# Attention and two MLP layers on one core: split inputs kept in DRAM for the wide tiles, and six weight chunks decoded through PSUM

## The chip, the core and the metric

The kernel runs on one core of a Trainium2 chip. The metric is the device time in microseconds of one execution. Three timed runs of the kernel before took 1110.44, 1110.76 and 1112.65 us (median 1110.76). One more execution was profiled; it took 1110.38 us.

## The reference

Four batches of eight heads of attention (576 rows, 64 columns a head) are mixed with a linear memory term, and go through two MLP layers of 2304 tokens, 512 model columns and 2048 hidden columns:

```python
scores = where(causal, -1e9, q @ k.T / 8); a = softmax(scores)
q_p = elu(q) + 1
attn = sigmoid(beta) * (q_p @ M_prev) / (q_p . z_prev + 1e-6) + (1 - sigmoid(beta)) * (a @ v)
x = attn laid out as (2304, 512)
x1 = elu(x @ moe_w_in) @ moe_w_out
out = leaky_relu(x1 @ moe2_w_in) @ moe2_w_out
```

The MLP weights arrive as float64, read as pairs of 32-bit integers. Tokens and weights are each split into a high part and a low remainder, both of a type that TensorE takes in one pass, and a product is the sum of three matmuls: high by high, low by high, high by low.

## The kernel before

**Order.** The program is written in units (a tile of scores, one chunk of an MLP layer, a load). A scheduler that simulates the program with costs of its own fixes the order of the instructions on every engine when the kernel is built. On the chip each engine, and SyncE's queue, which issues all DMAs, then runs its list strictly in order.

**Weights.** The 2048 hidden columns are 16 chunks `f` of 128. `load_w` fetches a chunk's two integer blocks, `wraw` (512 KB each, two buffers), and makes the pair `w`. It has two forms. Where `pools["decode_bank"]` names a PSUM bank, it works on halves of 128x512 through that one bank: ScalarE L112, VectorE L113, L114, L117, ScalarE's cast (helper `copy`, L242), VectorE L121 for the low part. A half keeps the bank from its first step to its last, so the next half starts behind it. Otherwise it works on the whole chunk of 128x1024 in the SBUF tile `wm` (one buffer): ScalarE L126, VectorE L127, L128, L131, ScalarE's cast, and GpSimd L137 twice for the low part.

**Attention with the first layer's narrow part.** The first seven chunks (`NFA`) are decoded during the first batch, by the PSUM form through bank `po`. Tokens come in eight parts of 288 (`pi` 0 to 7). As soon as the attention of a batch is through, its two parts' units are woven into the attention of the next: `u_x` makes the input x of a part, `u_h` one chunk's hidden block (12 matmuls in a PSUM bank, then `elu`: ScalarE L631, L632, VectorE L633, and `g_split`: VectorE's cast to `gh`, L244, and GpSimd's `gl`, L626), `u_o` the seven chunks' share of the output, stored as `ys`. For parts 2 to 7 `u_x` loads two halves of x, adds them on VectorE (L682), stores the sum as `xs` (L683), and splits it (`split_x`): ScalarE casts `xh`, GpSimd subtracts `xl` (L612). Parts 0 and 1 have their x in `xm` already.

**Between attention and the wide part.** From about 410 us the last parts' units run, merged with the loads of six more chunks (`merge(side, wun[:NPRE])`, L782), which use the SBUF form. The remaining three are loaded inside the first wide tile.

**Wide part.** The nine other chunks, 7 to 15, run over tiles of 512 tokens (four, and one of 256). `load2` gets a tile's x 256 tokens at a time through the one buffer `x`, and splits it into `xw`, `xv`: ScalarE casts `xw` (L242) and GpSimd subtracts `xv` (L806). Two sets of `xw`, `xv` alternate. Hidden blocks go to banks `tp` and `pm` in turn (two of each, so the fifth chunk, f = 11, needs the bank that the ELU of f = 7 has read). The tile's four output blocks use three `sc` banks and `po`. At a tile's end VectorE adds `ys` (L852), and the sums are stored as `x1s` (L853) from the two buffers `st`. Then the second layer runs over all 16 chunks, with its own loads (L818) and the same `load_x`.

Of the kernel before, what the change touches and what calls it, by code (L numbers as in the profile page):

```python
# [8 lines left out]
F32 = mybir.dt.float32  # L9
F32R = mybir.dt.float32r  # L10
# [5 lines left out]
P = 128  # L16
# [3 lines left out]
def _f(ap):  # L20
    return ap.bitcast(F32)
# [3 lines left out]
def kernel(  # L25
# [14 lines left out]
    nc = tc.nc  # L40
# [4 lines left out]
    NKC = DM // P  # L45
# [6 lines left out]
    V32 = 1  # L52
# [7 lines left out]
    TN = 256  # L60
# [87 lines left out]
    def halves(n):  # L148
# [5 lines left out]
    xq_scr = [  # L154
        [dram.tile([P, NKC, tile_tok(t)[1]], F32, name=f"xq{i}_{j}") for j in range(2)] for i, t in enumerate(tiles1)
    ]
    x_scr = [
        xm_scr[t][:, :, o:o + w] if t < V32 else dram.tile([P, NKC, w], F32, name=f"xs{i}")
        for i, (t, o, w, _) in enumerate(parts)
    ]  # L160
    y_scr = [dram.tile([P, NKC, p[2]], F32, name=f"ys{i}") for i, p in enumerate(parts)]
    x1_scr = [dram.tile([P, NKC, TN], F32, name=f"x1s{i}") for i in range(NTT)]

# [497 lines left out]
    def phase1_units(ti):  # L661

        units = []
        for pi, (pt, o, w, _) in enumerate(parts):
            if pt != ti:
                continue
            st = {}

            def u_x(pi=pi, o=o, w=w, st=st):
                xt = mtile("x", 1, F32, (NKC, NW))[:, :, 0:w]  # L670
                if ti < V32:
                    nc.sync.dma_start(xt, xm_scr[ti][:, :, o:o + w])
                    st["x"] = split_x(xt, w, pi % 2)
                    st["g"] = {}
                    return
                x2 = mtile("y", 1, F32, (NKC, NW))[:, :, 0:w]
                for j in range(2):
                    ps, pz = slice(64 * j, 64 * j + 64), slice(64 - 64 * j, 128 - 64 * j)
                    nc.sync.dma_start(xt[ps], xq_scr[ti][j][ps, :, o:o + w])
                    nc.sync.dma_start(x2[ps], xq_scr[ti][j][pz, :, o:o + w])  # L680
                for c in range(NKC):
                    nc.vector.tensor_tensor(out=xt[:, c], in0=xt[:, c], in1=x2[:, c], op=ALU.add)  # L682
                nc.sync.dma_start(x_scr[pi], xt)  # L683
                st["x"] = split_x(xt, w, pi % 2)
                st["g"] = {}

            def u_h(f, w=w, st=st):
                ph = h_bank()[:, 0:w]
                h_mm(ph, wi_tiles[0, f], *st["x"])
                st["g"][f] = elu(ph, w)  # L690

            def u_o(ec, pi=pi, w=w, st=st):
                py = bank("sc" if tail else "pm")[:, 0:w]
                o_mm(py, range(NFA), 0, ec, st["g"], 0, NFA - 1)
                y = mtile("st", 2)[:, 0:w]
                copy(E_Y, y, py)
                nc.sync.dma_start(y_scr[pi][:, ec], y)

            units.append((0, u_x))
            for f in range(NFA):  # L700
                units.append((HC * 12 * w / 2.4, lambda f=f, u=u_h: u(f)))
            for ec in range(NKC):
                units.append((3 * NFA * w / 2.4, lambda ec=ec, u=u_o: u(ec)))
        return units
# [74 lines left out]

    wun = [(1, lambda f=f: load_w(0, wpb, w1i, w1o, f, f - NFA)) for f in range(NFA, NF)]  # L780
    tail = True
    merge(side, wun[:NPRE])  # L782
    wun = wun[NPRE:]
    w2 = [lambda f=f: load_w(1, wpa, w2i, w2o, f, f) for f in range(NFA)]
    w2 += [lambda f=f: load_w(1, wpb, w2i, w2o, f, f - NFA) for f in range(NFA, NF)]
# [5 lines left out]

    n_wide = 0

    def load_x(fetch, t0, n):

        nonlocal n_wide
        par = n_wide % 2
        n_wide += 1
        xh = mtile(f"xw{par}", 1, F32R, (NKC, TW))[:, :, 0:n]
        xl = mtile(f"xv{par}", 1, F32R, (NKC, TW))[:, :, 0:n]  # L800
        for o in range(0, n, TN):
            xt = mtile("x", 1, F32, (NKC, TN))
            fetch(xt, t0 + o)
# [8 lines left out]
    wide = [(t0, min(TW, NT - t0)) for t0 in range(0, NT, TW)]  # L812

    def load2(t0, n):
        return load_x(lambda xt, t: recut(xt, x_scr, t, TN), t0, n)

    def load3(t0, n):
        return load_x(lambda xt, t: nc.sync.dma_start(xt, x1_scr[t // TN]), t0, n)  # L818
# [104 lines left out]
```

## Time and profile before

| | kernel before |
|---|---|
| median of 3 runs, us | 1110.76 |
| profiled execution, us | 1110.38 |
| its span, first to last instruction, us | 1108.6 |
| TensorE busy, us | 1062.3 (96%) |
| VectorE busy, us | 600.1 (54%) |
| GpSimd busy, us | 563.7 (51%) |
| ScalarE busy, us | 493.6 (45%) |
| mean granted clock of TensorE | 0.989 |

In the rows, PE is TensorE, DVE is VectorE, ACT is ScalarE, POOL is GpSimd and SP is SyncE. L12 is line 12 of the kernel. A row `out<-in` names what is written and read. PEclk is the granted clock as a share of the full 2.4 GHz; at about 0.5 it is the lower level of 1.2 GHz. Idle time in brackets is that of the same engine just before the instruction, with what ended it.

### The profile page before, as it was taken

Reading aid. Unit: us, or ns where it says so; the run is one execution under the profiler, and the core shown is the slowest. Engines: PE = TensorE matmul, PEld = TensorE weight load, DVE = VectorE, ACT = ScalarE, POOL = GpSimd, SP = SyncE. Lnnn points to the kernel's source line nnn. Section 1 sums busy time; section 2 is a strip of 40 time slices with the busy share of each in tenths; the row PEclk is TensorE's granted clock in tenths of the full one; section 3 lists DMA queues with packets and bytes.
Section 4 is the critical chain, followed back from the end, with each engine's and each line's share of the span. In section 5 each row is a group of like instructions: output and inputs, shape, how many; then the busy total and the mean of one; then the engine's idle time right before and its main releaser. Section 6 shows DMA issues by size and latency. Waiting matters only on the chain.

```text
span 1108.6 us, 17441 instructions
## 1 busy us (share of the span) xinstructions
PE 1062.3 (96%) x5904; PEld 916.4 (83%) x5904; DVE 600.1 (54%) x1398; ACT 493.6 (45%) x1205; POOL 563.7 (51%) x710
## 2 busy tenths in 40 slices
PE   6998899999989998979999999999999999999997
PEld 3877799989979998967777889888888888888896
DVE  6889978787869837656565223655222232132232
ACT  5898878687858635444343223432111111111110
POOL 7676785775747527666575224855322322222222
PEclk9999999999999999989999999999999999999999
DMA  7654533744462147543635113431200100010010
GB/s 180 186 144 96 135 89 92 174 112 116 109 171 80 51 150 225 158 140 124 201 115 168 56 40 96 152 114 38 67 10 1 48 29 1 1 39 1 1 38 20
DMA packets 145912, 104.43 MB, mean 94 GB/s; under 512 B 81440, under 2 KB 139808, under 8 KB 145824
## 3 DMA queue, kind: packets, MB, share of 16 engines
q1 hardware_dynamic: 145824, 103.33, 32.4%
q8 instruction: 47, 0.77, 0.3%
q14 instruction: 41, 0.34, 0.1%
HBM read 73.80 MB, written 25.95 MB: 90 GB/s over the span
## 4 chain that ended last, share of the span: by engine, by line
PE 69%; DMA 8%; DVE 8%; POOL 6%; issue 4%; ACT 3%; SPq 2%; DVEq 0%; POOLq 0%; ACTq 0%
PE pm L619 16%; PE sc L871 14%; PE tp L619 12%; PE sc L647 5%; PE po L871 4%; PE po L525 4%; PE pm L647 4%; PE tp L458 3%; POOL xv L806 2%; PE sc L429 2%; POOL w L137 1%; PE po L647 1%; PE sc L430 1%; DMA wraw<-in_moe_w_out_dram 1%; DMA x1s<-st 1%
## 5 line engine op out<-in xcount | busy, mean ns | idle before, releaser
L626 POOL TENSOR_TENSOR gl<-e,gh 128x512 fp32r<-128x512 f32 (+2 forms) x181 | 202.7, 1123 | 358.3 <-DVE gh L244 314.6
L619 PE MATMUL tp<-xw,w 128*128 128x512 f32 (+1 forms) x504 | 147.1, 374 | 5.6 <-DVE e L633 5.6
L619 PE MATMUL pm<-xw,w 128*128 128x512 f32 (+1 forms) x496 | 143.9, 372 | 0.0
L871 PE MATMUL sc<-w,gh 128*128 128x512 f32 x448 | 137.7, 393 | 0.0
L647 PE MATMUL sc<-gh,w 128*128 128x512 f32 (+2 forms) x438 | 108.6, 347 | 5.7 <-DVE st L852 2.9
L619 PEld LDWEIGHTS tp<-xw,w 128*128 128x128 f32 x504 | 92.2, 190 | 24.3 <-DVE e L633 6.0
L452 POOL TENSOR_SCALAR pt<-pt,rs,omg 128x128 f32<-128x128 f32 (+4 forms) x160 | 102.0, 646 | 19.6 <-DVE rs L447 18.1
L619 PEld LDWEIGHTS pm<-xw,w 128*128 128x128 f32 x496 | 90.5, 188 | 18.4
L437 ACT ACTIVATE pt<-pt,mx 128x128 f32<-128x128 f32 (+4 forms) x160 | 93.3, 584 | 24.9 <-DVE mx L432 23.4
L871 PEld LDWEIGHTS sc<-w,gh 128*128 128x128 f32 x448 | 83.1, 188 | 17.9
L619 PE MATMUL tp<-xv,w 128*128 128x512 f32 (+1 forms) x252 | 94.1, 374 | 0.0
L619 PE MATMUL pm<-xv,w 128*128 128x512 f32 (+1 forms) x248 | 92.0, 371 | 0.0
L647 PEld LDWEIGHTS sc<-gh,w 128*128 128x128 f32 x438 | 75.6, 190 | 17.7 <-issue 3.8
L638 ACT ACTIVATE e<-pm 128x512 f32<-128x512 f32 (+1 forms) x40 | 22.2, 555 | 151.6 <-PE pm L619 151.6
L619 PE MATMUL pm<-xh,w 128*128 128x288 f32 x368 | 82.1, 309 | 5.9 <-DVE e L633 4.5
L244 DVE CAST gh<-e 128x512 fp32r<-128x512 f32 (+2 forms) x146 | 76.2, 524 | 20.6 <-PE po L647 8.0
L458 PE MATMUL tp<-ident,pt 128*128 128x128 f32 x480 | 81.7, 276 | 5.4 <-DVE dl L251 2.0
L871 PE MATMUL sc<-w,gl 128*128 128x512 f32 x224 | 85.4, 393 | 0.0
L639 DVE TENSOR_TENSOR e<-tp,e 128x512 f32<-128x512 f32 (+1 forms) x40 | 25.5, 636 | 107.7 <-ACT e L638 107.6
L639 DVE TENSOR_TENSOR e<-pm,e 128x512 f32<-128x512 f32 (+1 forms) x40 | 25.5, 637 | 106.9 <-ACT e L638 106.9
L137 POOL TENSOR_TENSOR w<-wm,w 128x512 fp32r<-128x512 f32 x50 | 66.2, 1343 | 30.1 <-ACT w L242 30.1
L638 ACT ACTIVATE e<-tp 128x512 f32<-128x512 f32 (+1 forms) x40 | 22.1, 553 | 117.4 <-PE tp L619 117.2
(155 smaller groups left out, 2509.1 us busy)
## 6 DMA issues: line engine op xcount, KB each, us to landing
wraw<-in_moe_w_in_dram SPq DMA_DIRECT2D x32, 512.0 KB, 4.1
wraw<-in_moe_w_out_dram SPq DMA_DIRECT2D x32, 512.0 KB, 4.9
ys<-st SPq DMA_DIRECT2D x32, 144.0 KB, 3.1
x1s<-st SPq DMA_DIRECT2D x36, 128.0 KB, 1.8
x<-x1s SPq DMA_DIRECT2D x9, 512.0 KB, 3.7
out_dram<-st SPq DMA_DIRECT2D x36, 128.0 KB, 1.7
vn<-in_v_dram SPq DMA_DIRECT2D x64, 64.0 KB, 2.4
xq<-xp SPq DMA_DIRECT2D x24, 160.0 KB, 2.0
```

The lines of the kernel that those rows point to most:

```text
L137: nc.gpsimd.tensor_tensor(out=w[:, 1, a], in0=t[:, a], in1=_f(w)[:, 0, a], op=ALU.subtract)
L244: (nc.vector if eng == "V" else nc.gpsimd).tensor_copy(dst, src)
L437: nc.scalar.activation(out=pt[0:m, 0:nk], in_=pt[0:m, 0:nk], func=AF.Exp, scale=-1.0, bias=mx[0:m, last:last + 1], accum_out=self.pd["ss"] ...
L452: nc.gpsimd.tensor_scalar(out=pt, in0=pt, scalar1=rs[0:m, i:i + 1], scalar2=omg[0:m, h:h + 1], op0=ALU.mult, op1=ALU.mult,)
L458: nc.tensor.transpose(dst, self.p[c][:, k0:k0 + kn], ident)
L525: nc.tensor.matmul(po[:, a:b], w, x, start=i == 0, stop=i == len(mms) - 1)
L619: nc.tensor.matmul(ph, wi[:, wj, kc, :], xx[:, kc, :], start=n_mm == 0, stop=n_mm == 11)
L626: nc.gpsimd.tensor_tensor(out=gl, in0=g, in1=_f(gh), op=ALU.subtract)
L638: nc.scalar.mul(t, ph, 0.01)
L639: nc.vector.tensor_tensor(out=t, in0=ph, in1=t, op=ALU.max)
L647: nc.tensor.matmul(py, wo[:, wj, ec * P:(ec + 1) * P], gg, start=opens and f == first and n_mm == 0, stop=closes and f == last and n_mm == 2,)
L871: nc.tensor.matmul(pos[tb], gg[:, tb * P:(tb + 1) * P], wo[:, wj, :], start=f == 0 and n_mm == 0, stop=f == NF - 1 and n_mm == 2,)
```

## The change

`u_x` stores both parts of the split, `xh` and `xl`, as the DRAM tensors `xp_scr` for all eight parts, and no longer the sum `xs`: 16 stores of 576 KB in place of six. `load2` then fetches `xw` and `xv` of a wide tile straight from them, by four to six DMAs of 2 MB in all for 512 tokens; the copy through the buffer `x`, ScalarE's casts and GpSimd's subtractions are left out in the first layer's wide tiles and stay in the second layer's. Apart from that, the six chunks between attention and the wide part are decoded by the PSUM form, through bank `po`.

```diff
--- before.py
+++ after.py
@@ -154,10 +154,7 @@
     xq_scr = [
         [dram.tile([P, NKC, tile_tok(t)[1]], F32, name=f"xq{i}_{j}") for j in range(2)] for i, t in enumerate(tiles1)
     ]
-    x_scr = [
-        xm_scr[t][:, :, o:o + w] if t < V32 else dram.tile([P, NKC, w], F32, name=f"xs{i}")
-        for i, (t, o, w, _) in enumerate(parts)
-    ]
+    xp_scr = [[dram.tile([P, NKC, p[2]], F32, name=f"x{n}{i}") for i, p in enumerate(parts)] for n in "hl"]
     y_scr = [dram.tile([P, NKC, p[2]], F32, name=f"ys{i}") for i, p in enumerate(parts)]
     x1_scr = [dram.tile([P, NKC, TN], F32, name=f"x1s{i}") for i in range(NTT)]
 
@@ -667,11 +664,16 @@
             st = {}
 
             def u_x(pi=pi, o=o, w=w, st=st):
+                def split():
+                    st["x"] = split_x(xt, w, pi % 2)
+                    for n in range(2):
+                        nc.sync.dma_start(xp_scr[n][pi], _f(st["x"][n]))
+                    st["g"] = {}
+
                 xt = mtile("x", 1, F32, (NKC, NW))[:, :, 0:w]
                 if ti < V32:
                     nc.sync.dma_start(xt, xm_scr[ti][:, :, o:o + w])
-                    st["x"] = split_x(xt, w, pi % 2)
-                    st["g"] = {}
+                    split()
                     return
                 x2 = mtile("y", 1, F32, (NKC, NW))[:, :, 0:w]
                 for j in range(2):
@@ -680,9 +682,7 @@
                     nc.sync.dma_start(x2[ps], xq_scr[ti][j][pz, :, o:o + w])
                 for c in range(NKC):
                     nc.vector.tensor_tensor(out=xt[:, c], in0=xt[:, c], in1=x2[:, c], op=ALU.add)
-                nc.sync.dma_start(x_scr[pi], xt)
-                st["x"] = split_x(xt, w, pi % 2)
-                st["g"] = {}
+                split()
 
             def u_h(f, w=w, st=st):
                 ph = h_bank()[:, 0:w]
@@ -779,7 +779,9 @@
 
     wun = [(1, lambda f=f: load_w(0, wpb, w1i, w1o, f, f - NFA)) for f in range(NFA, NF)]
     tail = True
+    pools["decode_bank"] = "po"
     merge(side, wun[:NPRE])
+    pools["decode_bank"] = None
     wun = wun[NPRE:]
     w2 = [lambda f=f: load_w(1, wpa, w2i, w2o, f, f) for f in range(NFA)]
     w2 += [lambda f=f: load_w(1, wpb, w2i, w2o, f, f - NFA) for f in range(NFA, NF)]
@@ -791,13 +793,15 @@
 
     n_wide = 0
 
-    def load_x(fetch, t0, n):
-
+    def wide_x():
         nonlocal n_wide
         par = n_wide % 2
         n_wide += 1
-        xh = mtile(f"xw{par}", 1, F32R, (NKC, TW))[:, :, 0:n]
-        xl = mtile(f"xv{par}", 1, F32R, (NKC, TW))[:, :, 0:n]
+        return [mtile(f"{nm}{par}", 1, F32R, (NKC, TW)) for nm in ("xw", "xv")]
+
+    def load_x(fetch, t0, n):
+
+        xh, xl = (x[:, :, 0:n] for x in wide_x())
         for o in range(0, n, TN):
             xt = mtile("x", 1, F32, (NKC, TN))
             fetch(xt, t0 + o)
@@ -812,7 +816,10 @@
     wide = [(t0, min(TW, NT - t0)) for t0 in range(0, NT, TW)]
 
     def load2(t0, n):
-        return load_x(lambda xt, t: recut(xt, x_scr, t, TN), t0, n)
+        xs = wide_x()
+        for x, scr in zip(xs, xp_scr):
+            recut(_f(x), scr, t0, n)
+        return [x[:, :, 0:n] for x in xs]
 
     def load3(t0, n):
         return load_x(lambda xt, t: nc.sync.dma_start(xt, x1_scr[t // TN]), t0, n)
```

After the change the lines of the kernel move: L633 becomes L630, L631/L632 become L628/L629, L244 becomes L241, L242 becomes L239, L682 becomes L684, L790 becomes L792, L853 becomes L860.

VectorE, kernel before, at the end of the six chunks: `wm` is a chunk in the making, and the first `e` of width 512 is that of f = 7, which frees the bank for f = 11.

```order
L127 TENSOR_SCALAR wm<-wm 128x1024 [waits Activation_49]
L128 SCALAR_TENSOR_TENSOR wm<-wraw,wm 128x1024 [waits DMAHW1_49,DMAHW0_49,DVE_49]
L131 SCALAR_TENSOR_TENSOR wm<-wraw,wm 128x1024 [waits DVE_49]
L127 TENSOR_SCALAR wm<-wm 128x1024 [waits DVE_49,Activation_49]
L128 SCALAR_TENSOR_TENSOR wm<-wraw,wm 128x1024 [waits DMAHW1_49,DMAHW0_49,DVE_49]
L131 SCALAR_TENSOR_TENSOR wm<-wraw,wm 128x1024 [waits DVE_49]
L633 SCALAR_TENSOR_TENSOR e<-e,tp 128x512 [waits Activation_49]
L244 CAST gh<-e 128x512 [waits DVE_49,PE_49]
```

VectorE, kernel after, the same place: `po` is a half in the making, and the first `e` of width 512 is again that of f = 7.

```order
L121 TENSOR_TENSOR w_7173<-po,w_7173 128x512 [waits Activation_49]
L113 TENSOR_SCALAR po<-po 128x512 [waits Activation_49]
L114 SCALAR_TENSOR_TENSOR po<-wraw,po 128x512 [waits DMAHW0_49,DVE_49]
L117 SCALAR_TENSOR_TENSOR po<-wraw,po 128x512 [waits DVE_49]
L121 TENSOR_TENSOR w_7173<-po,w_7173 128x512 [waits Activation_49]
L113 TENSOR_SCALAR po<-po 128x512 [waits Activation_49]
L114 SCALAR_TENSOR_TENSOR po<-wraw,po 128x512 [waits DMAHW3_49,DVE_49]
L117 SCALAR_TENSOR_TENSOR po<-wraw,po 128x512 [waits DVE_49]
L630 SCALAR_TENSOR_TENSOR e<-e,tp 128x512 [waits Activation_49]
L630 SCALAR_TENSOR_TENSOR e<-e,pm 128x512 [waits Activation_49,Pool_49]
L241 CAST gh<-e 128x512 [waits DVE_49,PE_49,Pool_49]
```

The ELU of f = 7 stood behind the SBUF steps of all six chunks; it now stands behind ten whole halves and three of the four VectorE steps of the eleventh.

ScalarE, kernel before, the same place: `e` is the ELU of f = 7 and f = 8, `xw` the next wide tile's input.

```order
L242 CAST w_7141<-wm 128x1024 [waits DVE_49]
L631 ACTIVATE e<-tp 128x512
L631 ACTIVATE e<-pm 128x512
L242 CAST xw_7509<-x 128x256 [waits DMAHW2_49,DMAHW3_49,DMAHW0_49,Activation_49]
L242 CAST xw_7509<-x 128x256 x3
L632 ACTIVATE e<-e 128x512 [waits Activation_49]
L126 ACTIVATE wm<-wraw 128x1024 [waits DMAHW5_49,DMAHW4_49,Pool_49]
L632 ACTIVATE e<-e 128x512 [waits Activation_49]
```

ScalarE, kernel after, the same place.

```order
L112 ACTIVATE po<-wraw 128x512 [waits DMAHW0_49,DVE_49]
L239 COPY st<-sc 128x288 [waits DMAHW6_49,PE_49,Activation_49]
L239 CAST w_7173<-po 128x512 [waits DVE_49]
L112 ACTIVATE po<-wraw 128x512 [waits DMAHW3_49,DVE_49]
L628 ACTIVATE e<-tp 128x512 [waits PE_49]
L628 ACTIVATE e<-pm 128x512 [waits PE_49,Pool_49]
L629 ACTIVATE e<-e 128x512 [waits Activation_49] x2
```

Between the two steps of the ELU of f = 7 (L631 and L632) stood the four casts of `xw`, which wait for DMAs; they are gone, and the two steps follow each other.

SyncE, kernel before, at the switch from the first wide tile to the second: `x<-xs` is the input of the third tile and, behind the stores, of the fourth, `x1s<-st` the first tile's output, `y<-ys` what is added to its second half.

```order
L790 DMA x<-xs_94 128x4x160 [waits DMAHW2_49,DMAHW1_49,Pool_49]
L790 DMA x<-xs_95 128x4x96
L102 DMA wraw<-in_moe_w_in_dram 128x4x256 [waits DMAHW5_49,DMAHW6_49,DVE_49,Activation_49]
L106 DMA wraw<-in_moe_w_out_dram 128x1024
L853 DMA x1s_106<-st 128x256 [waits DVE_49] x2
L853 DMA x1s_106<-st 128x256 [waits DMAHW7_49,DVE_49]
L853 DMA x1s_106<-st 128x256 [waits DMAHW0_49,DVE_49]
L790 DMA y<-ys_98 128x4x32 [waits DMAHW1_49]
L790 DMA y<-ys_99 128x4x224 [waits DMAHW2_49]
L790 DMA x<-xs_95 128x4x192 [waits DMAHW3_49,Pool_49]
L790 DMA x<-xs_96 128x4x64 [waits DMAHW4_49]
L102 DMA wraw<-in_moe_w_in_dram 128x4x256 [waits DMAHW5_49,DVE_49,Activation_49]
```

SyncE, kernel after, the same place: `xw` and `xv` are now the third tile's input.

```order
L792 DMA xw_7910<-xh_95 128x4x128 [waits PE_49]
L792 DMA xw_7910<-xh_96 128x4x288
L792 DMA xw_7910<-xh_97 128x4x96
L792 DMA xv_7911<-xl_103 128x4x128 [waits PE_49]
L792 DMA xv_7911<-xl_104 128x4x288 [waits DMAHW0_49]
L792 DMA xv_7911<-xl_105 128x4x96 [waits DMAHW1_49]
L102 DMA wraw<-in_moe_w_in_dram 128x4x256 [waits DMAHW2_49,DVE_49,Activation_49]
L106 DMA wraw<-in_moe_w_out_dram 128x1024 [waits DMAHW3_49]
L860 DMA x1s_116<-st 128x256 [waits DMAHW4_49,DVE_49]
L860 DMA x1s_116<-st 128x256 [waits DMAHW5_49,DVE_49]
L860 DMA x1s_116<-st 128x256 [waits DMAHW6_49,DVE_49]
L860 DMA x1s_116<-st 128x256 [waits DMAHW7_49,DVE_49]
```

Ahead of the `wraw` loads and the first tile's stores stood two loads of x with 0.5 MB together; now six loads with 2 MB together stand there. The load of `y` comes behind the stores as before.

VectorE, kernel before, in attention: L682 adds the two halves of x of part 5, and `e` is the ELU of a hidden block that runs beside it.

```order
L432 ISA pt_5318,mx<-sc,mask 128x288 [waits PE_49]
L432 ISA mx 128x1
L682 TENSOR_TENSOR x<-x,y 128x288 [waits DMAHW6_49,DMAHW4_49,DMAHW7_49,DMAHW3_49,DMAHW1_49]
L633 SCALAR_TENSOR_TENSOR e<-e,pm 128x288 [waits Activation_49]
L682 TENSOR_TENSOR x<-x,y 128x288 x3
L303 TENSOR_TENSOR kl_0_152<-sc,kk_5273 64x320 [waits Activation_49]
```

VectorE, kernel after, the same place.

```order
L630 SCALAR_TENSOR_TENSOR e<-e,pm 128x288 [waits Activation_49]
L300 TENSOR_TENSOR kl_0_162<-sc,kk_5289 64x256 [waits Activation_49]
L248 TENSOR_TENSOR ac<-tp,ac 64x320 [waits Activation_49]
L529 COPY xp<-po 128x256 [waits DMAHW0_49,PE_49]
L248 TENSOR_TENSOR dl_146<-tp,dh_144 128x384 [waits Activation_49]
L429 ISA pt_5334,mx<-sc,mask 128x288 [waits PE_49]
L429 ISA mx 128x1
L684 TENSOR_TENSOR x<-x,y 128x288 [waits DMAHW5_49,DMAHW7_49,DMAHW4_49,DMAHW3_49]
L684 TENSOR_TENSOR x<-x,y 128x288 x3
L300 TENSOR_TENSOR kl_0_160<-sc,kk_5288 64x320 [waits Activation_49]
```

The ELU of that hidden block stood behind the first addition, which waits for DMAs; it now stands ahead of it, and the next block's ELU stands behind.

## Rows read from the trace of the kernel before

**Rows 1.** Stretches of the span (`us, engines busy us (x instructions), PEclk, DMA share, GB/s`).

```profile
130.00:410.00 280.00, 268.93 (x2034) 263.71 (x2034) 216.76 (x645) 201.40 (x577) 177.28 (x279) 0.98 0.42 110
410.00:480.00 70.00, 60.77 (x398) 56.17 (x397) 44.12 (x58) 36.36 (x75) 48.07 (x47) 0.98 0.65 207
520.00:560.00 40.00, 37.44 (x153) 29.44 (x152) 25.77 (x32) 16.67 (x25) 23.62 (x20) 0.96 0.53 159
600.00:1108.00 508.00, 502.86 (x2375) 416.74 (x2373) 156.04 (x286) 97.78 (x181) 176.81 (x162) 1.00 0.13 42
```

**Rows 2.** TensorE in the timeline, at idle times: `start us, us, ... [idle before <-releaser]`.

```profile
478.40 1.22 PE L619 MATMUL tp<-xw,w 128*128 128x512 f32 x2 [5.60 <-DVE e L633]
...
541.61 0.91 PE L647 MATMUL sc<-gh,w 128*128 128x512 f32 x2 [2.37 <-DVE st L852]
...
434.05 1.06 PE L647 MATMUL sc<-gh,w 128*128 128x288 f32 x6 [1.56 <-DVE gh L244]
...
226.40 0.41 PE L525 MATMUL po<-qph,ms 128*128 128x320 f32 x1 [2.66 <-DVE xp L532]
...
332.20 0.85 PE L619 MATMUL pm<-xh,w 128*128 128x288 f32 x2 [4.18 <-DVE e L633]
```

**Rows 3.** Timeline of ScalarE and VectorE around the longest of these.

```profile
475.77 1.32 ACT L242 CAST xw<-x 128x256 fp32r<-128x256 f32 x4 [2.69 <-DMA ys<-st]
477.00 0.62 ACT L632 ACTIVATE e<-e 128x512 f32<-128x512 f32 x1
...
477.66 0.69 DVE L633 SCALAR_TENSOR_TENSOR e<-e,tp 128x512 f32<-128x512 f32 x1 [6.64 <-ACT e L632]
```

**Rows 4.** Stretches again: four with a lower granted clock.

```profile
227.90:231.30 3.40, 3.40 (x18) 3.40 (x17) 3.31 (x9) 2.68 (x8) 2.28 (x5) 0.50 0.71 220
330.00:337.00 7.00, 4.80 (x20) 4.79 (x21) 5.62 (x14) 4.92 (x15) 4.37 (x7) 0.52 0.47 151
477.00:484.00 7.00, 5.60 (x13) 4.43 (x14) 6.24 (x8) 3.40 (x6) 4.96 (x6) 0.51 0.38 104
541.90:545.30 3.40, 3.40 (x9) 2.60 (x8) 1.18 (x2) 1.14 (x1) 0.68 (x1) 0.51 1.04 327
```

**Rows 5.** Groups of instructions in 410 to 480 us (`xcount | busy us, mean ns`).

```profile
L128 DVE SCALAR_TENSOR_TENSOR wm<-wraw,wm 128x1024 int32<-128x1024 int32 x6 | 9.3, 1551 | 0.2
L131 DVE SCALAR_TENSOR_TENSOR wm<-wraw,wm 128x1024 int32<-128x1024 int32 x6 | 8.1, 1345 | 0.1
L127 DVE TENSOR_SCALAR wm<-wm 128x1024 int32<-128x1024 int32 x7 | 5.6, 799 | 10.9 <-ACT wm L126 10.9
L137 POOL TENSOR_TENSOR w<-wm,w 128x512 fp32r<-128x512 f32 x12 | 15.8, 1333 | 9.1 <-ACT w L242 9.1
L244 DVE CAST gh<-e 128x288 fp32r<-128x288 f32 x14 | 10.2, 744 | 0.4
```

**Rows 6.** One line over the span: `duration ns min/median/max`.

```profile
L113 DVE TENSOR_SCALAR po<-po x14: 673/694/700, 10.4 to 89.9; 128x512 int32<-128x512 int32 x14
```

**Rows 7.** Timeline: two halves decoded through PSUM, and the first chunk through SBUF.

```profile
24.05 0.64 ACT L112 ACTIVATE po<-wraw 128x512 f32<-128x512 f32 x1 [2.85 <-DMA wraw<-in_moe_w_in_dram]
27.52 0.69 DVE L121 TENSOR_TENSOR w<-po,w 128x512 fp32r<-128x512 f32 x1 [0.65 <-ACT w L242]
...
88.81 0.63 ACT L112 ACTIVATE po<-wraw 128x512 f32<-128x512 f32 x1
94.75 0.68 DVE L121 TENSOR_TENSOR w<-po,w 128x512 fp32r<-128x512 f32 x1
...
413.77 1.15 ACT L126 ACTIVATE wm<-wraw 128x1024 f32<-128x1024 f32 x1 [0.93 <-DMA wraw<-in_moe_w_out_dram]
```

**Rows 8.** Timeline around the switch from the first tile to the second: SyncE and VectorE.

```profile
527.14 8.67 SPq L853 DMA_DIRECT2D x1s<-st  x4
...
541.04 0.76 DVE L852 TENSOR_TENSOR st<-sc,y 128x256 f32<-128x256 f32 x2 [1.77 <-issue]
```

**Rows 9.** Timeline of VectorE during attention, ahead of the idle time at 332 us.

```profile
331.32 0.46 DVE L682 TENSOR_TENSOR x<-x,y 128x288 f32<-128x288 f32 x1 [4.77 <-DMA xq<-xp]
```

## The prediction

> **What bounds the kernel now.** I read the table of stretches first. TensorE is busy for 268.93 of 280 us in most of attention, for 60.77 of 70 between attention and the wide part, and for 502.86 of 508 from 600 us on [rows 1]. Where TensorE is busy nothing of this change can be gained, so the last 508 us are set aside: what the change does there only lightens ScalarE and GpSimd, which are not the bound. The idle time worth looking at is the 9.2 us of 410 to 480, the 2.6 us of 520 to 560, and what attention has.
>
> Second, the timeline of TensorE, for the size and the releaser of its gaps. The largest is 5.60 us before 478.40, then 4.18 before 332.20, 2.66 before 226.40, 2.37 before 541.61 and 1.56 before 434.05 [rows 2]. All name VectorE, so the next view is what VectorE waited for. At 477.66 it runs the ELU of f = 7 after 6.64 us of idle time that ScalarE's L632 ended; ScalarE's L632 came at 477.00, behind four casts of `xw` that began at 475.77, after a wait for a DMA [rows 3]. TensorE's gap is thus not a lack of ELU speed: ScalarE, in order, held the ELU's second step behind an input for the *next* tile, whose memory was still being read by the store of `ys`.
>
> Third, the granted clock. After four of these gaps it stands at about 0.5, the level of 1.2 GHz: in 477 to 484 TensorE works 5.60 us at 0.51, in 541.9 to 545.3 3.40 us at 0.51, in 227.9 to 231.3 3.40 us at 0.50, in 330 to 337 4.80 us at 0.52 [rows 4]. Work at half the clock takes twice as long, so each of these stretches costs half of its busy time more: 2.8, 1.7, 1.7 and 2.4 us. A gap that goes should take its price with it.
>
> **The change part by part.** The sum starts at the profiled execution, 1110.38 us, which lies 0.4 under the median of the timed runs.
>
> *The casts and subtractions of the first layer's wide tiles go.* The order shows ScalarE's L631 and L632 of f = 7 next to each other. With the wait for the `ys` store off ScalarE, the gap of 5.60 us and its clock price of 2.8 go: -8.4. What is late next is counted below. The wait itself does not vanish: the direct load into `xw` waits for the same store, but in SyncE's queue. Queued behind it there are the load of `y` and the weights of f = 14; f = 13's weights are now ahead of it. The second tile wants its input some 50 us later, so this wait costs nothing; without that cover it would cost the 2.69 us that ScalarE waited [rows 3].
>
> *The six chunks go through PSUM.* On VectorE a chunk took 1.551 + 1.345 + 0.799 = 3.70 us [rows 5]. By the PSUM form it takes eight steps; one has a median of 0.694 us [rows 6], and L121 has 0.69 [rows 7], so 5.55 us. Over six chunks that is +11.1 us of VectorE, whose 44.12 busy us of 70 [rows 1] become 55. GpSimd loses 15.8 us (L137) [rows 5]. ScalarE has two passes of 0.64 us in place of one of 1.15 [rows 7], next to no change. TensorE sees this only through two things.
>
> The first is the chain through bank `po`. A half holds the bank from its L112 to the end of its L121: 24.05 to 28.21 = 4.16 us when little else runs, 88.81 to 95.43 = 6.62 us in the last of the first 14, beside attention [rows 7]. In the new order the ELU of f = 7 stands on VectorE behind ten halves and the first four steps of the eleventh, that is, the half less a cast and L121 (1.3 us). The first chunk's decoding began at 413.77 [rows 7]. With the mean of the two, 5.39 us, the ELU ends at 413.8 + 53.9 + 4.1 + 0.7 = 472.5. TensorE ran out of work at 478.40 - 5.60 = 472.8; with the small gaps ahead of it partly gone (next paragraph but one) it does so at 471.0. That leaves a new stall of 1.5 us: +1.5. The bounds: at 4.16 us a half the ELU is there at 459, no stall; at 6.62 it is there at 486.0, a stall of 15.0 us. I take the middle, since the stretch has less ScalarE work than attention (36.36 of 70 against 201.40 of 280 [rows 1]) and a VectorE that is as full (55 of 70 against 216.76 of 280).
>
> What the rows show of the steps themselves: L113 stays within 673 and 700 ns over the span though GpSimd works beside it [rows 6], while the two like steps of the SBUF form have means of 1551 and 1345 ns [rows 5]. The Trainium skill ("SBUF — State Buffer", section "Who interferes with whom") says that VectorE and GpSimd share one port pair as an exclusive lock, and that a VectorE instruction with at most one SBUF input, outside the two-port modes, does not contend for it. By that rule the new steps are never blocked and a half stays near the short end, with no stall: the sum would be 1.5 us lower. The trace agrees on the steps, but the half at 88.81 took 6.62 us with steps of the same length [rows 7]: what made it long was waiting in the queues, which the rule does not take away. So I keep the 1.5.
>
> The second is VectorE's queue: each `gh` cast and ELU of the last parts now stands between more steps, one of which waits for ScalarE's cast inside each half. The gap of 1.56 us at 434.05 [rows 2] is the nearest row of such a wait; the bounds are 0 and the whole +11.1 us. I take +1.0.
>
> *The other gaps in 410 to 480.* Of 9.2 us idle, 3.6 are not the large gap. They are waits on VectorE, ScalarE and GpSimd in turn, in queues which hold `xw` casts, L806 and L137 now and not after. I count half of them as gained: -1.8 (bounds 0 and -3.6).
>
> *The switch from the first wide tile to the second.* TensorE's 2.37 us wait for VectorE's `st` [rows 2]; the addition waits for the load of `y` [rows 8], which SyncE issues only behind the four `x1s` stores, 8.67 us long at 527.14 [rows 8]. In the new order there are 2 MB of `xw`/`xv` ahead of those stores where there were 0.5 MB. They wait for TensorE alone and no more for GpSimd and the buffer `x`, so they can start when the first tile's last hidden block is read, some 8 us before its last output block is done. With the clock price the gap is worth 4.1 us; I take half of it, -2.0. Bounds: -4.1, and +4.8, since the 1.5 MB more take 4.8 us at the 327 GB/s of full engines [rows 4].
>
> *Attention.* The 16 stores of 576 KB, the stores of `xl` that wait in SyncE's queue for GpSimd (with loads of the next heads behind them), and the scheduler's new order are all that changes. At 332 TensorE waits for an ELU that stands behind an addition which waits 4.77 us for DMAs [rows 9]. The order now puts that ELU ahead of the addition and the next one behind. There are two `pm` banks, so one more hidden block of 12 matmuls covers 1.6 us of the wait (attention's 2034 matmuls take 268.93 us, 0.13 each [rows 1]): -1.6. Bounds: -11 (both gaps of attention with their clock prices, 4.4 and 6.6) and +7 (another gap like the one at 332).
>
> Sum: 1110.38 - 8.4 + 1.5 + 1.0 - 1.8 - 2.0 - 1.6 = 1099.1.
>
> **The rivals.**
>
> *More goes than I count.* The new order in attention also takes the gap at 226 (2.66 + 1.7) and what I left at 332 (4.18 - 1.6 + 2.4). For it: both gaps stand behind additions of x in VectorE's queue, and both additions have moved. Against: the additions still wait for the same DMAs, and there are more DMAs. 1099.1 - 4.4 - 5.0 = 1089.7.
>
> *The tile switch gets worse.* The 2 MB collide with stores and `y`; the gap at 541 stays and grows by 4.8 us. For it: in 541.9 to 545.3 the DMA engines are at 1.04 of their time [rows 4]. Against: the early start. 1099.1 + 2.0 + 4.8 = 1105.9.
>
> *Slower: the chain through bank `po` sets the pace.* Place: VectorE's ELU of f = 7 behind the eleventh half, at about 486. With 6.62 us a half, TensorE stalls for 15.0 us and pays 2.8 of clock again: 1099.1 - 1.5 + 15.0 + 2.8 = 1115.4. For it: one bank, six steps that alternate between two engines, VectorE at 55 of 70. Against: halves of 4.16 us are in the trace. It decides from the half at which the new stall and its clock price make up for the 12.8 us gained without it, a stall of 10.0: 11 halves in 67.8 us, 6.2 us each.
>
> *Nothing moves.* The change does not do what it says: the released ScalarE is not what TensorE waits for next, because the ELU now waits in VectorE's queue as long as it waited before (5.6 us, with clock), and the rest cancels. 1110.
>
> **How the numbers follow.** Forecast 0.50, with a range of its own of 1094 to 1104; more goes 0.14; the tile switch 0.15; the chain 0.14; nothing 0.07. A change of 0.2% (2.2 us) is about what a measurement can tell from none. Faster: 0.49 + 0.14 + 0.13, and 0.01 of the chain's short end, 0.77. Same: 0.05 of nothing, 0.03 of the chain, 0.02 of the switch, 0.10. Slower: 0.13. The range runs from 1088, below the second case, to 1111: it leaves out the chain's upper part and the tail of the second case.
>
> **What would show it.** Right: no gap of over 2 us before the first matmul of f = 11, a granted clock of 1.0 in the 10 us after it, halves of 5 to 5.7 us from about 414 to 478, VectorE near 55 of 70 us there, ScalarE's two ELU steps of f = 7 side by side. Wrong: a gap of TensorE there with VectorE's ELU as releaser and halves over 6 us (the chain); a longer gap at the switch with full DMA engines; no gap and a faster attention (more goes); or a start of the first half much later than 414, since every time above counts from there.

## The result, and the profile after

The changed kernel took 1097.47, 1102.11, 1102.78 and 1102.60 us (median 1102.36) beside 1110.44 to 1112.65 of the kernel before: a ratio of 0.9912, 95% interval 0.9884 to 0.9940. Measured again in the first set of experiments it took 1099.59 us, ratio 0.9882 (0.9860 to 0.9904). The forecast was 1099.1 us. The profiled execution took 1097.47 us, the fastest of the first four.

The stretches of the kernel after, with the columns of [rows 1]:

```profile
130.00:410.00 280.00, 265.98 (x2016) 258.90 (x2015) 218.81 (x644) 202.22 (x576) 178.09 (x279) 0.99 0.46 123
410.00:480.00 70.00, 69.31 (x452) 64.75 (x452) 54.44 (x94) 37.32 (x80) 24.34 (x27) 1.00 0.81 261
520.00:560.00 40.00, 39.27 (x169) 31.24 (x169) 23.98 (x32) 17.03 (x22) 20.68 (x16) 1.00 0.51 165
600.00:1095.00 495.00, 489.76 (x2319) 406.22 (x2317) 152.57 (x280) 94.30 (x173) 168.88 (x154) 1.00 0.13 43
```

Between attention and the wide part TensorE's idle time falls from 9.2 us to 0.7, and the clock stays at 1.00. VectorE is busy for 54.4 us there (55 was forecast), GpSimd for half of what it was.

At the place of the gap of 5.60 us [rows 2, 3], TensorE's first matmul of f = 11 starts without a wait. ScalarE runs the ELU's steps side by side, and VectorE's step has ended at 467.6 us, 2.8 us ahead of that matmul:

```profile
470.37 0.63 PE L616 MATMUL tp<-xw,w 128*128 128x512 f32 x2
...
464.76 0.58 ACT L628 ACTIVATE e<-tp 128x512 f32<-128x512 f32 x1
465.24 0.58 ACT L628 ACTIVATE e<-pm 128x512 f32<-128x512 f32 x1
465.71 1.15 ACT L629 ACTIVATE e<-e 128x512 f32<-128x512 f32 x2
...
466.93 0.68 DVE L630 SCALAR_TENSOR_TENSOR e<-e,tp 128x512 f32<-128x512 f32 x1
```

The decode steps and the `gh` cast in 410 to 480 us, against [rows 5]:

```profile
L113 DVE TENSOR_SCALAR po<-po 128x512 int32<-128x512 int32 x12 | 8.4, 697 | 4.9 <-ACT po L112 4.7
L121 DVE TENSOR_TENSOR w<-po,w 128x512 fp32r<-128x512 f32 x12 | 8.3, 690 | 4.3 <-ACT w L239 4.2
L241 DVE CAST gh<-e 128x288 fp32r<-128x288 f32 x14 | 6.3, 453 | 0.7 <-DVE e L630 0.5
```

The four decode steps stay at 0.69 us each, as forecast. The mean of the `gh` casts fell from 744 to 453 ns, which was not forecast: VectorE got 3.9 us back there. Single casts show where from. The kernel before, VectorE, then GpSimd:

```profile
420.25 0.77 DVE L244 CAST gh<-e 128x288 fp32r<-128x288 f32 x1
429.58 0.30 DVE L244 CAST gh<-e 128x288 fp32r<-128x288 f32 x1
...
419.29 1.57 POOL L626 TENSOR_TENSOR gl<-e,gh 128x288 fp32r<-128x288 f32 x2 [4.24 <-DVE gh L244]
430.05 0.86 POOL L626 TENSOR_TENSOR gl<-e,gh 128x288 fp32r<-128x288 f32 x1 [3.71 <-DVE gh L244]
```

Where GpSimd runs beside a cast for a sixth of its time at most, the cast takes 0.30 us; where it runs beside it for most of the time, one took 0.68 to 1.37 us in the kernel before and 0.62 to 0.95 in the kernel after. In this stretch four of the 14 casts were of the short kind before, and ten after.

At the switch from the first wide tile to the second (against the gap of 2.37 us and [rows 8]), on SyncE, VectorE and TensorE:

```profile
510.41 4.07 SPq L792 DMA_DIRECT2D xv<-xl  x3
...
517.45 6.85 SPq L860 DMA_DIRECT2D x1s<-st  x4
524.35 1.20 SPq L792 DMA_DIRECT2D y<-ys  x2
...
529.47 0.76 DVE L859 TENSOR_TENSOR st<-sc,y 128x256 f32<-128x256 f32 x2 [1.87 <-issue]
...
530.04 0.71 PE L644 MATMUL sc<-gh,w 128*128 128x512 f32 x2 [0.73 <-DVE st L859]
```

The loads of 2 MB are issued by 514.5 us, 3.0 us before the first store. The order of waits is the old one, but the gap is 0.73 us, and the granted clock stays at 1.00 in 520 to 560.

Where the time went is best seen by the start of the n-th matmul, counted from 0 in each trace (5904 in all of them):

| start of matmul, us | before | after | after, again | split only | PSUM only | cast on GpSimd | stores by ScalarE |
|---|---|---|---|---|---|---|---|
| 2500th (end of attention) | 388.2 | 391.0 | 393.0 | 393.7 | 388.0 | 388.1 | 388.1 |
| 3000th | 463.6 | 460.1 | 461.8 | 464.5 | 461.4 | 463.6 | 457.4 |
| 3250th | 528.6 | 518.2 | 519.8 | 521.9 | 519.8 | 523.4 | 514.6 |
| 3750th | 651.4 | 638.2 | 640.5 | 639.9 | 646.8 | 646.2 | 632.5 |
| execution, us | 1110.38 | 1097.47 | 1100.32 | 1100.19 | 1107.20 | 1104.81 | 1093.12 |

From the 2500th to the 3750th the changed kernel gains 16.0 us, and up to the 2500th it loses 2.8. At the 2500th, 3250th and 3750th every kernel of the table has put the same number of columns through TensorE. At the 3000th their orders differ, by up to 1.7 us of work, so that row is a rough one. Each column is one execution.

### The profile page after: what moved, and what is told of

Read it like the earlier page. It is cut to its first block, busy times and chain, and to the rows that moved or that the text cites. A ratio compares the mean times of both kernels' runs of the same rounds, so it can differ in the third digit from the quotient of the medians.

```text
span 1095.7 us, 17443 instructions
## 1 busy us (share of the span) xinstructions
PE 1056.0 (96%) x5904; PEld 910.5 (83%) x5904; DVE 605.1 (55%) x1428; ACT 485.3 (44%) x1181; POOL 512.5 (47%) x662
## 4 chain that ended last, share of the span: by engine, by line
PE 74%; DVE 9%; DMA 8%; POOL 2%; ACT 2%; issue 2%; SPq 2%; DVEq 0%; ACTq 0%; POOLq 0%
PE pm L616 16%; PE sc L878 14%; PE tp L616 13%; PE sc L644 7%; PE pm L644 4%; PE po L878 4%; PE tp L455 3%; PE po L522 3%; PE pm L522 3%; DMA x<-xq 2%; DMA wraw<-in_moe_w_out_dram 2%; PE po L644 2%; PE sc L426 1%; POOL w L137 1%; PE sc L427 1%
## 5 line engine op out<-in xcount | busy, mean ns | idle before, releaser
L623 POOL TENSOR_TENSOR gl<-e,gh 128x512 fp32r<-128x512 f32 (+2 forms) x181 | 198.0, 1096 | 400.2 <-DVE gh L241 324.9
L449 POOL TENSOR_SCALAR pt<-pt,rs,omg 128x128 f32<-128x128 f32 (+4 forms) x160 | 102.6, 650 | 26.6 <-DVE rs L444 24.3
L241 DVE CAST gh<-e 128x512 fp32r<-128x512 f32 (+2 forms) x146 | 72.7, 499 | 18.0 <-PE po L644 5.0
L429 DVE CUSTOM_DVE_ANT_0 pt<-sc,mask 128x128 f32<-128x128 f32 (+4 forms) x160 | 69.2, 446 | 8.3 <-PE sc L427 3.9
```

The source lines that it names most:

```text
L241: (nc.vector if eng == "V" else nc.gpsimd).tensor_copy(dst, src)
L429: nc.vector.tensor_tensor_reduce(out=pt[0:m, k0:k0 + n], in0=sc[0:m, 0:n], in1=mk, op0=ALU.add, op1=ALU.min, scale=-0.125, scalar=mx[0:m, ...
L449: nc.gpsimd.tensor_scalar(out=pt, in0=pt, scalar1=rs[0:m, i:i + 1], scalar2=omg[0:m, h:h + 1], op0=ALU.mult, op1=ALU.mult,)
L623: nc.gpsimd.tensor_tensor(out=gl, in0=g, in1=_f(gh), op=ALU.subtract)
```

## The experiments

The theory to be tested was the prediction's: casts of `xw` in ScalarE's queue make the large gap. Its rival: the SBUF form of the decode, with its chain through `wm` and GpSimd, makes it. Each ratio is against the kernel before, run beside it. The sets ran on different chips, so across sets the ratios are compared and not the medians.

**The changed kernel again.** No edit.

> The changed kernel again, nothing altered, to see what parts its executions (1097.5 us in the profiled one, 1102.1 to 1102.8 in three others). Theory: the 5 us lie in attention, before 410 us, as gaps of TensorE with the lower granted clock behind them; from 410 to 560 us the idle time stays under 2 us in either kind. Rival: they lie in 410 to 560 us, where the DMA engines are at 0.8 of their time and a late transfer can bring a gap back. Time expected: median 1102, profile between 1097 and 1103.

Median 1099.59 us, 1095.86 to 1100.41. Its profile, at 1100.32 us, is 2.0 us behind the first one at the 2500th matmul and 2.3 at the 3750th. So most of what parts these two executions, 2.0 of 2.8 us, arises in attention, as expected; 410 to 560 us have 1.2 us of idle time here. The second one has four stretches of 3.4 us at a granted clock of 0.50 in attention, from 142.9, 224.8, 245.3 and 340.9 us, behind or within gaps of 1.96 us, 1.57 with 1.05, 2.60, and 3.22. The first has nearly the same gaps, but only one such stretch, from 337.3.

**Either half of the change alone.** The first leaves out the line that sets the decode bank; the second adds only that to the kernel before:

```diff
-    pools["decode_bank"] = "po"
     merge(side, wun[:NPRE])
```

> The stored split inputs alone; the six chunks keep the SBUF form. Theory (the gap of 5.6 us at 472 comes from ScalarE's casts of xw standing before the ELU of f = 7): the gap before the first matmul of f = 11 is under 1.5 us, no lower clock behind it, and the time is 8 to 10 us under the kernel before (1101 to 1103). Rival (the SBUF form's chain through wm and GpSimd is what makes the stretch slow): a gap of 4 us or more stays there, and the time is within 3 us of the kernel before.

1096.70 us, ratio 0.9874 (0.9851 to 0.9897): all of the gain, and below the 1101 to 1103 that was expected. The gap before f = 11 is 0.93 us, with the clock at 1.00.

> The PSUM form for the six chunks alone; the wide tiles load and split x as before, and in its order the four casts of xw still stand between the two ScalarE steps of the ELU of f = 7. Theory: a gap of 3 to 6 us before the first matmul of f = 11 stays, released by the ELU, with the lower clock behind it; time 1106 to 1111. Rival: the decode was the cause, the gap goes, 1099 to 1103.

1104.47 us, ratio 0.9938 (0.9917 to 0.9959): half of the gain, a time between the two ranges that were expected, and TensorE has no gap before f = 11. The theory is wrong in this. The casts still stand between the two steps of the ELU, but in its trace they no longer wait (ScalarE, then SyncE):

```profile
464.86 0.58 ACT L631 ACTIVATE e<-tp 128x512 f32<-128x512 f32 x1
465.67 1.33 ACT L242 CAST xw<-x 128x256 fp32r<-128x256 f32 x4 [0.24 <-DMA ys<-st]
466.91 0.63 ACT L632 ACTIVATE e<-e 128x512 f32<-128x512 f32 x1
...
463.06 1.11 SPq L697 DMA_DIRECT2D ys<-st  x2
```

The `ys` store went out at 463.1. In the kernel before it went out at 471.5. It stood on SyncE behind a load of weights, whose buffer the decode's L131 read until 471.02, and it needed ScalarE's copy into `st`, which stood behind the decode's L126. The kernel before, ScalarE, VectorE, then SyncE in the timeline:

```profile
466.64 1.14 ACT L126 ACTIVATE wm<-wraw 128x1024 f32<-128x1024 f32 x1 [2.05 <-POOL w L137]
468.95 0.79 ACT L242 COPY st<-sc 128x288 f32<-128x288 f32 x2 [1.18 <-DMA ys<-st]
471.05 1.05 ACT L242 CAST w<-wm 128x1024 fp32r<-128x1024 f32 x1 [1.31 <-DVE wm L131]
472.01 0.58 ACT L631 ACTIVATE e<-tp 128x512 f32<-128x512 f32 x1
...
469.79 1.23 DVE L131 SCALAR_TENSOR_TENSOR wm<-wraw,wm 128x1024 int32<-128x1024 int32 x1
...
471.05 0.38 SPq L102 DMA_DIRECT2D wraw<-in_moe_w_in_dram  x1
471.52 0.46 SPq L697 DMA_DIRECT2D ys<-st  x1
```

So the wait that I named was the last of a row: ScalarE stood behind GpSimd's L137, this held `st`, the store and the first step of the ELU back to 472, and only then came the casts with a wait for that late store. This kernel loses part of its gain again with new gaps of TensorE in 528 to 589 us (1.21, 0.84 and 2.65 us, the last with a stretch of the lower clock behind it).

**The casts of one tile moved to GpSimd**, in the kernel before, nothing else touched:

```diff
-                copy(E_XH, xh[:, c, o:o + TN], xt[:, c])
+                copy("P" if n_wide == 2 else E_XH, xh[:, c, o:o + TN], xt[:, c])
```

> The kernel before with one edit: the eight casts of xw of the second wide tile run on GpSimd, so that nothing stands between ScalarE's two steps of the ELU of f = 7. Decode and loads are as before. Theory: the gap of 5.60 us falls under 1.5 us and the lower clock behind it goes; time 1110.8 - 8.4 = 1102, up to 1105 if GpSimd is late with the low parts. Rival (decode): gap and time as before, 1109 to 1112.

1107.36 us, ratio 0.9963 (0.9947 to 0.9979). The gap falls from 5.60 to 1.58 us and the lower clock behind it is gone (ScalarE, then TensorE):

```profile
472.09 0.58 ACT L631 ACTIVATE e<-tp 128x512 f32<-128x512 f32 x1
472.58 0.59 ACT L631 ACTIVATE e<-pm 128x512 f32<-128x512 f32 x1
473.05 0.63 ACT L632 ACTIVATE e<-e 128x512 f32<-128x512 f32 x1
...
474.46 0.73 PE L619 MATMUL tp<-xw,w 128*128 128x512 f32 x2 [1.58 <-DVE e L633]
```

L631 is at 472.1, where it was. So with the decode as it was, 4.0 of the 5.60 us go with the casts; with the clock price that is 6.8 us. The time of 1102 to 1105 was missed: the median gained 4.3, and 1.74 us of the rest stand in a new gap at 524 us, which GpSimd's `gl` ends.

**The stores alone**, added to the kernel before at both places of the split and never read (the line that makes `xp_scr` is left out here):

```diff
                 st["x"] = split_x(xt, w, pi % 2)
+                for n in range(2):
+                    nc.sync.dma_start(xp_scr[n][pi], _f(st["x"][n]))
```

> The kernel before with the 16 stores of xh and xl added in attention, never read; all else as before, xs stored too. It prices the stores by themselves. Theory (the 3 to 5 us that the changed kernel and the split-only one lose up to the 2500th matmul come from these stores in SyncE's queue, ahead of loads of x for which VectorE and then TensorE wait): the 2500th matmul 3 to 6 us later than the 388.2 us of before, time 1113 to 1117. Rival (the loss is chance of the scheduler's new order, or comes from parts that this kernel doesn't have): within 1 us of before at that matmul, time 1109 to 1112.

1120.91 us, ratio 1.0089 (1.0054 to 1.0124), more than expected. Its profile, from an execution of 1126.27 us, has the 2500th matmul at 400.2; 8.7 of the 12.0 us are lost from the 500th to the 700th, with gaps of 4.92 and 2.74 us. The gap before f = 11 has grown, with hardly a wait left at the casts, which shows the row of waits by itself (ScalarE, then TensorE; its lines stand further on, L632 is the ELU's first step):

```profile
486.87 1.12 ACT L126 ACTIVATE wm<-wraw 128x1024 f32<-128x1024 f32 x1 [2.29 <-POOL w L137]
487.89 0.59 ACT L632 ACTIVATE e<-tp 128x512 f32<-128x512 f32 x1
488.36 0.60 ACT L632 ACTIVATE e<-pm 128x512 f32<-128x512 f32 x1
488.87 1.32 ACT L243 CAST xw<-x 128x256 fp32r<-128x256 f32 x4
...
492.29 1.22 PE L620 MATMUL tp<-xw,w 128*128 128x512 f32 x2 [8.50 <-DVE e L634]
```

**The stores later, and by another engine.** In the first and third kernel the two stores stand behind the part's fifth hidden block; in the second and fourth ScalarE issues them at their old place (the diff), and the last is the second again:

```diff
-                        nc.sync.dma_start(xp_scr[n][pi], _f(st["x"][n]))
+                        nc.scalar.dma_start(xp_scr[n][pi], _f(st["x"][n]))
```

> The changed kernel with the two stores of a part moved from the split to behind the part's fifth hidden block, so that SyncE never waits for GpSimd's subtractions there and the next loads are issued ahead of the stores. Theory (place in SyncE's queue): the 2500th matmul comes 2 to 4 us earlier than in the changed kernel's 391 to 393, time 1095 to 1098. Rival (the bytes and issue time of 16 stores, wherever they stand): no change, 1099 to 1101.

1100.43 us, ratio 0.9903 (0.9873 to 0.9933), 2500th matmul at 392.6: no better than the changed kernel. This later place in the queue does not help.

> The changed kernel with the 16 stores issued by ScalarE instead of SyncE. Theory (SyncE's queue is what is full): the loads of x come earlier, the 2500th matmul 1 to 3 us earlier, 1097 to 1099; ScalarE pays for waiting on GpSimd's xl, which could take all of it back. Rival (bytes): no change in attention.

1094.45 us, ratio 0.9850 (0.9823 to 0.9878), 2500th matmul at 388.1: better than expected.

> The split-only kernel (six chunks in the SBUF form) with the late stores. Candidate for the best. Theory: the wide part as in the split-only kernel, attention 2 to 4 us better: 1093 to 1096. Rival: as the split-only kernel, 1096 to 1098.

1097.90 us, ratio 0.9870 (0.9838 to 0.9901): as the split-only kernel, so the theory of a better attention fails here too (2500th matmul at 393.4).

> The stored split inputs alone (six chunks in the SBUF form), with the 16 stores issued by ScalarE. Theory: the wide part as in the split-only kernel, attention as in the kernel with ScalarE's stores (2500th matmul at 388 to 389): 1092 to 1095, no worse than that kernel's 1094.5, since the PSUM form adds nothing once the casts are gone. Rival (the PSUM form is worth 2 us or more beside the stores): 1096 to 1098.

1099.56 us, ratio 0.9904 (0.9874 to 0.9934), 2500th matmul at 393.2: a miss. The time lies past the rival's, and by the ratios this kernel is 0.5% slower than the one with the PSUM form beside the same stores. The stretch from the 2500th to the 3750th matmul shows 0.8 to 2.1 us of that (246.6 us against 245.8 and 244.5 in that kernel's two profiles). In attention this execution is 2.3 us late by the 500th matmul already, and it loses 4.6 from the 1200th to the 1500th, where the other two lose 4.0 and 3.3.

> The changed kernel with the 16 stores issued by ScalarE, once more, since the same edit gave nothing to the split-only kernel (1099.6 against 1096.7). Theory (it is this kernel's order in attention, not the queue as such, that is good): the same trace again, 2500th matmul at 388 to 390, no step L391 over 0.5 us, 1094 to 1097. Rival (the first measurement was a good moment of the chip): 1098 to 1101, as the changed kernel.

1096.10 us, ratio 0.9849 (0.9810 to 0.9888): the ratio holds, and it is the lowest found, though its interval overlaps that of the split-only kernel. The trace is not the same again: the 2500th matmul is at 391.7, and one step L391 took 0.77 us. Two executions of this one kernel are 3.6 us apart there, so 388.1 alone is no sign of a better attention.

**The small step of VectorE at 137 us.** One of attention's new gaps has an odd row. VectorE's L391, on 128x10 elements, with a median of 0.17 us in this kernel, took 3.58 us beside GpSimd's back-to-back subtractions, and TensorE stood still (kernel after: VectorE, GpSimd, TensorE):

```profile
136.63 3.58 DVE L391 SCALAR_TENSOR_TENSOR den<-den,ging 128x10 f32<-128x10 f32 x1
...
135.57 3.11 POOL L609 TENSOR_TENSOR xl<-x,xh 128x288 fp32r<-128x288 f32 x4
138.65 1.53 POOL L623 TENSOR_TENSOR gl<-e,gh 128x288 fp32r<-128x288 f32 x2
...
140.67 0.55 PE L455 MATMUL tp<-ident,pt 128*128 128x128 f32 x3 [1.81 <-DVE al L248]
```

The edit writes the step with a scalar column in place of the second tensor, once for each of two heads:

```diff
-            gb = ging[:, 2 * hp:2 * hp + 2].unsqueeze(1).to_broadcast([P, ncs, 2])
-            nc.vector.scalar_tensor_tensor(out=den, in0=den, scalar=1e-6, in1=gb, op0=ALU.add, op1=ALU.mult)
+            for j in range(2):
+                g1 = ging[:, 2 * hp + j:2 * hp + j + 1]
+                nc.vector.tensor_scalar(
+                    out=den[:, :, j], in0=den[:, :, j], scalar1=1e-6, scalar2=g1, op0=ALU.add, op1=ALU.mult
+                )
```

> The changed kernel with VectorE's L391, a step of 128x10 with two SBUF inputs, written as two steps with one SBUF input and a scalar column each. In the changed kernel one such step took 3.58 us at 136.6, beside GpSimd's back-to-back subtractions of xl, and TensorE's gap of 1.81 us ended with what stood behind it. Theory (VectorE waits for the port that GpSimd holds, because the step reads two SBUF tensors): the step stays under 0.5 us, the gap at 139 goes, 1097 to 1099, 1 to 3 us under the changed kernel. Rival (VectorE waits for something else there, a semaphore that the trace doesn't show): a step of 3 us or more and the gap stay, 1099 to 1102.

1109.41 us, ratio 0.9985 (0.9965 to 1.0005). The remedy failed. Two of the new steps took 4.41 us together, again until GpSimd's row of subtractions ended (VectorE, then GpSimd):

```profile
140.63 4.41 DVE L392 TENSOR_SCALAR den<-den,ging 128x5 f32<-128x5 f32 x2
...
141.75 2.31 POOL L612 TENSOR_TENSOR xl<-x,xh 128x288 fp32r<-128x288 f32 x3
144.03 0.79 POOL L626 TENSOR_TENSOR gl<-e,gh 128x288 fp32r<-128x288 f32 x1
```

The new order of attention cost more than any gap (2500th matmul at 400.4), so this run says nothing of the price. That VectorE waits for GpSimd there fits both traces; which port or rule it is stays open, since the scalar column lies in the same memory. The profiles of the other kernels place the step. A step of 3.56 to 4.53 us stands in all seven profiles with stores issued by SyncE and the step as it was; in the six with stores by ScalarE or without them the longest is 0.96 us.

**Longer halves**, two steps more in each:

```diff
-                nc.vector.tensor_scalar(out=m, in0=m, scalar1=3, scalar2=None, op0=ALU.logical_shift_left)
+                for sh in (1, 1, 1) if tail else (3,):
+                    nc.vector.tensor_scalar(out=m, in0=m, scalar1=sh, scalar2=None, op0=ALU.logical_shift_left)
```

> The changed kernel with two more VectorE steps in each half of the six chunks (the shift by 3 as three shifts by 1), which lengthens a half from about 4.3 to 5.7 us. It tests the slower case that was priced beforehand: the chain through one bank decides from a certain half on. In the changed kernel the ELU of f = 7 ends at 467.6 and TensorE wants it at about 471. Theory: ten and a half halves longer by 1.4 us put it at 482, a stall of about 11 us, part of it taken by a later start of what stands ahead, so 6 to 12 us slower: 1106 to 1112. Rival (the chain has much slack, or the ELU moves ahead of the halves in the new order): under 3 us slower, 1099 to 1103.

1110.52 us, ratio 0.9992 (0.9968 to 1.0016): the prediction's slower case is real, with the whole gain gone, but at another place. The scheduler put the ELU of f = 7 ahead of the end of the chain, and the stall came later, at the weights of f = 12, whose cast ScalarE's L240 is (TensorE in the timeline):

```profile
491.35 0.79 PE L617 MATMUL pm<-xw,w 128*128 128x512 f32 x1 [7.98 <-ACT w L240]
```

Ten halves here take from 417.16 (the first L112) to 486.12 (the end of the tenth step L121, which is L122 in this kernel), 6.9 us each; in the changed kernel from 413.43 to 464.15, 5.1 us each. VectorE is no busier than there (53.0 of the 70 us from 410, against 54.4), which points at the length of the chain and not at VectorE's load.

## Why the prediction came out

*The large gap and its clock, -8.4.* Right in size: gap and lower clock are gone. Incomplete in the cause: the casts are a part of it (4.0 us, by the run that moved them), not the whole. I read the last releaser, a DMA, and one queue. The runs show two waits in a row in ScalarE's queue, both set by the slow decode, so that either half of the change removes most of the gap: split alone 0.9874, PSUM alone 0.9938, both 0.9882. I had credited the split inputs alone and taken the PSUM form as a cost; by itself it is a gain of 0.6%. Beside the split inputs the runs don't settle its worth: with SyncE's stores the two ratios are 0.9882 and 0.9874, with ScalarE's 0.9850 and 0.9849 against 0.9904.

*The chain through `po`, +1.5.* The halves took 5.1 us instead of 5.39 and the first began at 413.4, so the ELU was done 4.9 us before the forecast 472.5, and no stall came. The threshold of 6.2 us for the slower case stays untested as a number: at 6.9 us the gain was gone, by a stall at f = 12.

*VectorE's queue, +1.0, and the small gaps, -1.8.* 3.6 us of small idle times became 0.7: -2.9 in place of -0.8. The term that was mis-sized is VectorE's load: the +11.1 us are there, but the casts beside them got faster by 3.9 us as GpSimd's busy time fell from 48.1 to 24.3 us. The Trainium skill ("SBUF — State Buffer", section "Who interferes with whom") has the rule for this, that casts can take the port pair that GpSimd shares. The trace agrees, with 0.30 us for a cast alone and 0.62 to 1.37 beside GpSimd. I applied it to the new steps alone; the old casts are where it paid. And I set the new steps' 0.69 us beside 1.55 and 1.35 of the SBUF form without saying that those are twice as wide: their shortest take 1.21 and 1.20 us.

*The tile switch, -2.0.* It gave 1.6 us of gap and the clock's 1.7. The loads did start early enough.

*Attention, -1.6.* Wrong in sign: +2.8 and +4.8 us in the two profiles. The step at 332 itself held: from the 2000th to the 2500th matmul the changed kernel gains 1.1 and 2.1 us. What failed is that everything else in attention was put at nothing. From the 500th to the 700th it loses 1.9 and 2.5 us, with the new gap at 139, and from the 1200th to the 1500th 1.8 and 2.9, where the one gap of 2.66 us [rows 2] has become three, of 1.38, 1.05 and 2.47. The last of these is again an ELU behind an addition of x (kernel after, VectorE, then TensorE; the same at 332 on the last lines):

```profile
242.07 0.83 DVE L684 TENSOR_TENSOR x<-x,y 128x288 f32<-128x288 f32 x2 [1.95 <-DMA qn<-in_q_dram]
242.82 0.45 DVE L630 SCALAR_TENSOR_TENSOR e<-e,pm 128x288 f32<-128x288 f32 x1
...
243.32 0.53 PE L616 MATMUL pm<-xh,w 128*128 128x288 f32 x2 [2.47 <-DVE e L630]
...
334.54 2.17 DVE L684 TENSOR_TENSOR x<-x,y 128x288 f32<-128x288 f32 x4 [2.95 <-DMA kn<-in_k_dram]
...
337.52 0.85 PE L616 MATMUL pm<-xh,w 128*128 128x288 f32 x2 [2.92 <-DVE e L630]
```

The kernels without the stores have the 2500th matmul at 388.0 to 388.2. Those with stores issued by SyncE have it at 391.0 to 393.7 where attention is not edited further, and at 400.2 where `xs` is stored as well; with stores by ScalarE it is at 388.1, 391.7 and 393.2. So the kernels with stores are mostly 3 to 5 us later there. The scheduler's new order came with the stores in each of them, so that the price of the stores and that of the order are not told apart. One part is seen: the long step of VectorE at 137 us. With ScalarE's stores it is absent, and the loss from the 500th to the 700th matmul is 0.3 to 0.6 us in all three profiles. The rest stays open.

In all, -11.3 us were forecast; -12.9 were measured in the profile and -9 to -12 in the medians. The number came out in part by luck: three errors of 1.3 to 2.1 us on the good side met one of 4.4 on the bad side; 1.1 us of the profile's gain I can't assign.

## What to carry to other kernels

A releaser in a trace is the last wait of a row: before a gap is put down to it, ask why that thing was itself late, one queue further back. Two edits that each remove a gap do not add up when it is the same gap, so run each alone before keeping both. And a store that no engine waits for can still come at a price: the changed kernel, with its 16 stores and the order that came with them, gave back 2.8 to 4.8 us in attention of the 16 us gained behind it.

## What had not been expected of the hardware

A step of VectorE on ten elements a partition took 3.58 us where its median is 0.17. It began beside the second of six GpSimd subtractions in a row (four at 135.57, two at 138.65) and ended with the last of them. Seven profiles show the like, and in another kernel two steps on five elements took 4.41 us. The times fit a VectorE that is held for a whole series of GpSimd's instructions and not for one; what holds it is not shown.

And nearly the same gap does not always cost the clock. Behind a gap of 2.47 us at 243 the granted clock stayed at 1.00 in one execution of the changed kernel; at a gap of 2.60 in its place it stood at 0.50 in another. The gap in the second, then a stretch of the first and one of the second (`us, TensorE busy us (x matmuls), PEclk, DMA share, GB/s`):

```profile
245.67 0.85 PE L616 MATMUL pm<-xh,w 128*128 128x288 f32 x2 [2.60 <-DVE e L630]
...
243.00:248.00 5.00, 4.46 (x32) 1.00 0.31 121
...
245.30:248.70 3.40, 3.03 (x12) 0.50 0.01 2
```
